# Taking a decode kernel's last output out of PSUM in one VectorE copy, and sending it row by row from partitions 32 apart

## Chip, cores, metric

One core of one Trainium2 chip. The metric is the device time of one execution in microseconds, median of several runs. Runs of one kernel mostly agree within about 0.3%. The experiments ran on several chips, so each is compared with the kernel before in the same rounds. Beside the time, each kernel has one profiled execution with its trace. "SyncE", "ScalarE", "VectorE", "TensorE" and "GpSimd" are SP, ACT, DVE, PE and POOL in the profile's lines. In this kernel TensorE's sums lie in PSUM and all other tiles in SBUF, over up to 128 partitions (rows) each; transfers go between SBUF and HBM. An "issue" is the instruction with which SyncE or ScalarE starts a transfer; DMA engines then move its packets, and it has "landed" when the last update of its semaphore has come.

## The reference

A decode step for two batch rows with 576 features: layer norm, attention over the last 2048 entries of a cache (32 query heads, 16 key and value heads), and beside it a squared-ReLU block, both added to the input.

```python
xn = _layernorm(x, axis=-1)
return x + _A_ref(xn, A_k_cache, A_v_cache, A_wq, A_wo) + _B_ref(xn, B_w1, B_b1, B_w2, B_b2)
# _B_ref: h = xn @ w1 + b1;  r = where(h > 0, h, 0);  out = (r * r) @ w2 + b2      w2: (4608, 576)
# out: (2, 1, 576) bf16
```

Only the very end matters here: the last rows of `w2` are multiplied in, and 2x576 values leave PSUM for HBM.

## The kernel before

B = 2, D = 576, OH = 288, OQ = 144, P = 128, FR = 9. The last weights arrive in two transfers, 7 and 2 of 9 row groups. The last sums are kept in four quarters of 144 columns, one for each 32-partition quadrant of a PSUM bank, with a small matmul for each:

```python
    def mlp_tail(r0, r1):
        w2_sb = w2_tiles.pop((NG4 - 1, r0))
        for r in range(r0, r1):
            o = (r - r0) * D
            for i in range(4):
                pe_mm(mlp["out"][32 * i:32 * i + B, :], lhsT=mlp["h"][:, (NG4 - 1) * FR + r, :],
                                 rhs=w2_sb[:, o + i * OQ:o + (i + 1) * OQ], start=False, stop=(r == FR - 1),
                                 skip_group_check=True, tile_position=(0, 32 * i))
    # ... (cut: the stream of K, V and weights, and everything computed from it)
    mlp["out"] = psum.tile([P, OQ], F32, tag="misc", name="tail_ps")
    for i in range(4):       # the sums so far open the four quarters
        pe_mm(mlp["out"][32 * i:32 * i + B, :], lhsT=ident_f[0:B, 0:B], rhs=part[:, i * OQ:(i + 1) * OQ],
              start=True, stop=False, skip_group_check=True, tile_position=(0, 32 * i))
    mlp_tail(*W2P[NG4 - 1][1:])
    mlp_tail(*W2P[NG4][1:])

    for i, (cp, eng) in enumerate(((nc.vector.tensor_copy, nc.sync), (nc.scalar.copy, nc.scalar))):
        fin_sb = work.tile([B, OH], BF16, tag="fin", name=f"fin_sb_{i}")
        for q in range(2):
            k = 2 * i + q
            cp(out=fin_sb[:, q * OQ:(q + 1) * OQ], in_=mlp["out"][32 * k:32 * k + B, :])
        eng.dma_start(out=out2d[:, i * OH:(i + 1) * OH], in_=fin_sb[:])
```

Of the kernel before, what the change touches and what calls it, by code (L numbers as in the profile page):

```python
# [8 lines left out]
F32 = mybir.dt.float32  # L9
BF16 = mybir.dt.bfloat16  # L10
# [6 lines left out]
def kernel(  # L17
# [14 lines left out]
    nc = tc.nc  # L32
    P = 128
    B, Sq, D = A_x.shape
# [33 lines left out]
    OH = D // 2  # L68
    OQ = D // 4
# [4 lines left out]
    const = ctx.enter_context(tc.tile_pool(name="const", bufs=1))  # L74
# [3 lines left out]
    work = ctx.enter_context(tc.tile_pool(name="work", bufs=2))  # L78
# [3 lines left out]
    def pe_mm(out, **kw):  # L82
        return tc.keep_in_program_order(nc.tensor.matmul(out, **kw))  # L83
# [8 lines left out]
    out2d = out.rearrange("b s d -> (b s) d")  # L92
# [44 lines left out]
    for i in range(2):  # L137
        nc.scalar.dma_start(out=x_sb[B:B + 1, i * OH:(i + 1) * OH],
                            in_=B_b2[i * OH:(i + 1) * OH].rearrange("(o n) -> o n", o=1))
    eps_t = const.tile([B, 1], F32, name="eps_t")  # L140
    nc.vector.memset(eps_t[:], 1e-5)
    warm = const.tile([B, 122], F32, name="warm")
    nc.scalar.activation(out=warm[:, 0:1], in_=eps_t[:], func=ACT.Sqrt)
    for f in issue_kv(k_tiles, A_k_cache, 0, "k"):
        f()
# [12 lines left out]
    ident_f = const.tile([P, P], F32, name="ident_f")  # L158
# [25 lines left out]
    for a in range(2):  # L184
        for r in range(NR2):
# [3 lines left out]
                          in_=pro_ps[:, 0:2 * NR2, :].rearrange("p (a r) b -> p r a b", a=2))  # L189
    nc.vector.tensor_copy(out=xnT[:, 1:HP:2, :, :],  # L190
                          in_=pro_ps[:].rearrange("p (a r) b -> p r a b", a=2)[:, 0:NR2 - 1, :, :])
# [16 lines left out]
                          in_=ident[0:TH, 0:TH].unsqueeze(1).to_broadcast([TH, NT * 32 // TH, TH]))  # L208
    par = const.tile([P, 2, 2, Dh // 2], BF16, name="par")
    for e in range(2):  # L210
        nc.gpsimd.tensor_copy(out=par[:, e, :, :],
                              in_=ident[:, e:Dh:2].unsqueeze(1).to_broadcast([P, 2, Dh // 2]))
# [3 lines left out]
    for k in range(2):  # L216
        for h in range(2):
# [5 lines left out]
                          in_=ident[0:NG4, 0:NG4].unsqueeze(2).to_broadcast([NG4, NG4, B]))  # L223
# [172 lines left out]
    mlp = {}  # L396
# [46 lines left out]
    part = const.tile([B, D], F32, name="part")  # L443
# [107 lines left out]
        cp(out=part[:, i * OH:(i + 1) * OH], in_=out_ps[32 * i:32 * i + B, :])  # L551
    mlp["out"] = psum.tile([P, OQ], F32, tag="misc", name="tail_ps")
    for i in range(4):
        pe_mm(mlp["out"][32 * i:32 * i + B, :], lhsT=ident_f[0:B, 0:B], rhs=part[:, i * OQ:(i + 1) * OQ],
              start=True, stop=False, skip_group_check=True, tile_position=(0, 32 * i))
    mlp_tail(*W2P[NG4 - 1][1:])
    mlp_tail(*W2P[NG4][1:])

    for i, (cp, eng) in enumerate(((nc.vector.tensor_copy, nc.sync), (nc.scalar.copy, nc.scalar))):
        fin_sb = work.tile([B, OH], BF16, tag="fin", name=f"fin_sb_{i}")  # L560
        for q in range(2):
            k = 2 * i + q
            cp(out=fin_sb[:, q * OQ:(q + 1) * OQ], in_=mlp["out"][32 * k:32 * k + B, :])
        eng.dma_start(out=out2d[:, i * OH:(i + 1) * OH], in_=fin_sb[:])


# [28 lines left out]
```

## Time and profile before

| | before |
|---|---|
| time, median of 3 runs | 134.1 us (134.0 to 134.14) |
| span of the profiled run | 132.2 us |
| last weights have landed | 129.09 us after the span's start |
| last cast has signalled | 130.09 us |
| SyncE's output transfer has landed | 131.41 us |

One view is added, busy time in five stretches of the tail: first the stretch, then its length, each engine's busy time with its number of instructions, the granted TensorE clock, the share of the DMA engines, GB/s.

```profile
129.09:130.09 1.00, 0.30 (x8) 0.10 (x7) 0.59 (x2) 0.54 (x2) 0.00 (x0) 1.00 0.00 0
130.09:130.86 0.77, 0.00 (x0) 0.00 (x0) 0.00 (x0) 0.00 (x0) 0.00 (x0) 1.00 0.00 0
130.86:130.96 0.10, 0.00 (x0) 0.00 (x0) 0.00 (x0) 0.00 (x0) 0.00 (x0) 1.00 0.09 23
130.96:131.41 0.45, 0.00 (x0) 0.00 (x0) 0.00 (x0) 0.00 (x0) 0.00 (x0) 1.00 0.00 0
131.41:132.20 0.79, 0.00 (x0) 0.00 (x0) 0.00 (x0) 0.00 (x0) 0.00 (x0) 0.98 0.00 0
```

Of the 3.16 us after the last weights, engines compute in the first microsecond alone. Then come 0.77 us in which transfers are issued, 0.10 us of packets, 0.45 us until they count as landed, and the close.

### The profile page before, as it was taken

What the parts mean: (1) busy time and instruction counts of PE and PEld (TensorE: products, weight loads), DVE (VectorE), ACT (ScalarE), POOL (GpSimd) and SP (SyncE); (2) the same over time, 40 slices, a digit from 0 to 9 for tenths busy, and PEclk for the clock granted to TensorE, in tenths of its full rate; (3) what the DMA queues carried; (4) which work ended last, traced back from release to release, by engine and by line L of the source; (5) the groups of instructions that cost most, each with busy time, mean ns of one, the idle gap of its engine ahead of it and who ended that gap; (6) DMA issues with size and microseconds to landing.
All of it is one profiled execution on the core that took longest, in us unless ns stands there. A gap on an engine that the chain in (4) does not pass through costs nothing.

```text
span 132.2 us, 2040 instructions
## 1 busy us (share of the span) xinstructions
PE 89.0 (67%) x830; PEld 54.7 (41%) x830; DVE 59.1 (45%) x150; ACT 44.2 (33%) x64; POOL 7.7 (6%) x26
## 2 busy tenths in 40 slices
PE   0069319789862967879889389789303996399761
PEld 0059202639521354744466064466003661155540
DVE  6944400224640019246675823778800358644011
ACT  2705401015700226438457145357100751200011
POOL 7700000001000001000010000010000000000000
PEclk9999995955999599689999977999985699959999
DMA  4999989999998999999999999999999999999950
GB/s 154 389 451 479 413 382 431 431 484 477 439 404 350 436 416 441 426 446 416 431 431 426 436 421 439 426 429 431 428 441 416 446 423 422 429 420 433 419 238 1
DMA packets 3632, 53.74 MB, mean 406 GB/s; under 512 B 412, under 2 KB 420, under 8 KB 680
## 3 DMA queue, kind: packets, MB, share of 16 engines
q1 hardware_dynamic: 3604, 53.61, 95.2%
q8 instruction: 6, 0.10, 0.3%
q10 hardware_dynamic: 20, 0.01, 0.0%
q14 instruction: 2, 0.02, 0.0%
HBM read 53.62 MB, written 0.00 MB: 405 GB/s over the span
## 4 chain that ended last, share of the span: by engine, by line
DMA 72%; PE 20%; DVE 2%; ACT 2%; issue 1%; SPq 1%; DVEq 0%; ACTq 0%
DMA k<-in_A_k_cache_dram 44%; DMA w<-in_B_w_dram 14%; DMA wq_sb<-in_A_wq_dram 13%; PE kT_ps L86 10%; PE sc_ps L83 4%; PE q_ps L83 3%; PE pv_ps L83 2%; PE qs_ps L83 1%; DVE kT L286 1%; ACT kT L284 1%; ACT pr L323 1%; PE sm L83 1%; DVE qrow L250 1%; SPq L105 0%; DVE qz L266 0%
## 5 line engine op out<-in xcount | busy, mean ns | idle before, releaser
L86 PE MATMUL kT_ps<-ident_f,k 128*128 128x128 f32 x256 | 41.4, 319 | 12.6 <-DMA k<-in_A_k_cache_dram 12.1
L284 ACT COPY kT<-kT_ps 128x1024 bf16<-128x1024 bf16 x32 | 31.9, 1011 | 36.8 <-PE kT_ps L86 34.0
L86 PEld LDWEIGHTS kT_ps<-ident_f,k 128*128 128x128 f32 x256 | 34.4, 165 | 21.9 <-issue 16.6
L286 DVE COPY kT<-kT_ps 128x1024 bf16<-128x1024 bf16 x32 | 22.1, 691 | 31.9 <-PE kT_ps L86 31.8
L83 PE MATMUL sc_ps<-kT,qz 128*32 128x512 bf16 x128 | 10.7, 418 | 4.5 <-DVE kT L286 2.8
L83 PE MATMUL pv_ps<-v,pT 128*32 128x512 bf16 x128 | 11.7, 435 | 1.0 <-DVE acc L358 0.8
L312 POOL PARTITION_ALL_REDUCE gmax<-m x8 | 2.9, 365 | 103.1 <-DVE m L310 103.1
L323 ACT ACTIVATE pr<-sc_ps,nb 128x512 bf16<-128x512 f32 x8 | 5.5, 687 | 7.9 <-DVE nb L320 7.9
L83 PEld LDWEIGHTS <-xnT 128*4 128x4 bf16 x90 | 2.9, 105 | 11.6 <-issue 11.0
L308 DVE TENSOR_REDUCE mx<-sc_ps 128x1 f32<-128x512 f32 x8 | 5.5, 683 | 3.1 <-PE sc_ps L83 3.1
L83 PE MATMUL q_ps<-wq_sb,xnT 128*4 128x512 bf16 x36 | 3.7, 592 | 4.5 <-DMA wq_sb<-in_A_wq_dram 4.5
L83 PEld LDWEIGHTS <-qz 128*32 128x32 bf16 x128 | 2.3, 98 | 10.1 <-DVE kT L286 6.3
L83 PE MATMUL h_ps<-w_sb,xnT 128*4 128x384 bf16 x54 | 3.9, 420 | 3.4 <-DMA w_sb<-in_B_w_dram 3.4
L358 DVE SCALAR_TENSOR_TENSOR mix<-pv_ps,own_j,mix 128x128 f32<-128x128 f32 x16 | 5.6, 352 | 0.6
L329 DVE STREAM_TRANSPOSE pT<-pr 128x512 bf16<-128x512 bf16 x8 | 5.6, 702 | 0.2 <-ACT pr L323 0.2
L86 PE MATMUL pro_ps<-ident,xs 2*128 2x2 bf16 x10 | 0.6, 164 | 7.6 <-DVE xs L180 7.6
L83 PE MATMUL out_ps<-wo_sb,ws 128*2 128x288 bf16 x64 | 5.1, 323 | 0.3 <-DVE ws L387 0.3
L83 PEld LDWEIGHTS <-pT 128*32 128x32 bf16 x128 | 2.9, 98 | 5.9 <-issue 3.5
L551 ACT COPY part<-out_ps 2x288 f32<-2x288 f32 x1 | 0.4, 389 | 13.5 <-PE out_ps L83 13.5
L83 PE MATMUL sm<-acc,tohead 128*64 128x129 f32 x16 | 3.7, 313 | 1.8 <-DVE acc L358 1.8
L431 DVE TENSOR_TENSOR hs<-hT_ps,hodd 128x20 f32<-128x20 f32 (+1 forms) x4 | 0.5, 172 | 9.2 <-ACT hodd L428 9.2
L83 PE MATMUL out_ps<-w,hT_sb 128*2 128x288 bf16 x54 | 3.8, 286 | 1.1 <-DMA w<-in_B_w_dram 1.1
(78 smaller groups left out, 58.2 us busy)
## 6 DMA issues: line engine op xcount, KB each, us to landing
k<-in_A_k_cache_dram SPq DMA_DIRECT2D x8, 2048.0 KB, 7.7
v<-in_A_v_cache_dram SPq DMA_DIRECT2D x8, 2048.0 KB, 16.9
w_sb<-in_B_w_dram SPq DMA_DIRECT2D x1, 5184.0 KB, 19.3
wq_sb<-in_A_wq_dram SPq DMA_DIRECT2D x1, 4608.0 KB
wo_sb<-in_A_wo_dram SPq DMA_DIRECT2D x2, 2304.0 KB
w<-in_B_w_dram SPq DMA_DIRECT2D x3, 1296.0 KB, 27.2
w<-in_B_w_dram SPq DMA_DIRECT2D x1, 1008.0 KB
w<-in_B_w_dram SPq DMA_DIRECT2D x1, 288.0 KB
```

The source lines that it names most:

```text
L83: return tc.keep_in_program_order(nc.tensor.matmul(out, **kw))
L86: return tc.keep_in_program_order(nc.tensor.transpose(**kw))
L250: nc.vector.tensor_copy(out=qrow[:, 0, :], in_=q_ps[0][0:RB, :])
L284: pin(nc.scalar.copy(out=dst, in_=src))
L286: pin(nc.vector.tensor_copy(out=dst, in_=src))
L308: pin(nc.vector.tensor_reduce(out=mx[:], in_=sc_ps, axis=AX.X, op=ALU.max))
L312: nc.gpsimd.partition_all_reduce(gmax[:], m2[:], channels=P, reduce_op=ReduceOp.max)
L323: pin(nc.scalar.activation(out=pr[:], in_=sc_ps, func=ACT.Exp, bias=nb[:], scale=scale, accum_out=acc[:, Dh:Dh + 1]))
L329: pin(nc.vector.transpose(out=pT[:].rearrange("p t m -> p (t m)"), in_=pr[:]))
L358: op = nc.vector.scalar_tensor_tensor(out=nx, in0=pv_ps[:, j, :], scalar=own_j[:, j:j + 1], in1=acc, op0=ALU.mult, op1=ALU.add)
L431: nc.vector.tensor_tensor(out=hs[:].rearrange("p (g r) b -> p r g b", g=NG4)[:, r0:r0 + n, g:g + 2, :], in0=even[:, :, g:g + 2, :], in1=od ...
L551: cp(out=part[:, i * OH:(i + 1) * OH], in_=out_ps[32 * i:32 * i + B, :])
```

## The change

The intent: one VectorE cast in place of two on each of two engines, on the path that sets the end. For that, all 128 partitions of the PSUM tile must have been written, so the opening matmuls get 32 output rows. The output then sits in partitions 32i + b, and each batch row goes out as four pieces from partitions 32 apart. The spare tile `warm` only keeps the addresses of the later tiles on the same multiple.

```diff
-    warm = const.tile([B, 122], F32, name="warm")
+    warm = const.tile([B, 114], F32, name="warm")
...
-        pe_mm(mlp["out"][32 * i:32 * i + B, :], lhsT=ident_f[0:B, 0:B], rhs=part[:, i * OQ:(i + 1) * OQ],
+        pe_mm(mlp["out"][32 * i:32 * (i + 1), :], lhsT=ident_f[0:B, 0:32], rhs=part[:, i * OQ:(i + 1) * OQ],
...
-    for i, (cp, eng) in enumerate(((nc.vector.tensor_copy, nc.sync), (nc.scalar.copy, nc.scalar))):
-        fin_sb = work.tile([B, OH], BF16, tag="fin", name=f"fin_sb_{i}")
-        for q in range(2):
-            k = 2 * i + q
-            cp(out=fin_sb[:, q * OQ:(q + 1) * OQ], in_=mlp["out"][32 * k:32 * k + B, :])
-        eng.dma_start(out=out2d[:, i * OH:(i + 1) * OH], in_=fin_sb[:])
+    fin_sb = const.tile([P, OQ], BF16, name="fin_sb")
+    nc.vector.tensor_copy(out=fin_sb[:], in_=mlp["out"][:])
+    for b, eng in enumerate((nc.sync, nc.scalar)):
+        eng.dma_start(out=out2d[b:b + 1, :].rearrange("o (i n) -> (o i) n", i=4), in_=fin_sb[b:P:32, :])
```

## The prediction

> **What bounds the kernel now.** I read the page first, for the kind of kernel it is: a decode step that streams 53.6 MB of cache and weights through one core.
>
> ```profile
> span 132.2 us, 2040 instructions
> PE   0069319789862967879889389789303996399761
> DMA  4999989999998999999999999999999999999950
> DMA 72%; PE 20%; DVE 2%; ACT 2%; issue 1%; SPq 1%; DVEq 0%; ACTq 0%
> ```
>
> The second and third of these lines are busy tenths in 40 slices of 3.3 us, the fourth is the chain that ended last. DMA is full until slice 38, and 72% of the chain are transfers. VectorE and ScalarE hold 2% each. The change touches only the last slice and a half, so what counts is the order of events there. Next I read the end of that chain in order of time (start us, us, what):
>
> ```profile
> 109.99 19.10 DMA w<-in_B_w_dram
> 129.09 0.04 issue
> 129.13 0.40 PE tail_ps L83 x8
> 129.53 0.05 ACT fin_sb L563
> 129.58 0.24 issue
> 129.82 0.27 ACT fin_sb L563
> ```
>
> The last weights land at 129.09, eight matmuls on them end at about 129.53, and the casts out of PSUM end at 130.09. The chain stops there, but the span goes on to 132.2, so I read the timeline of the tail (start us, us, engine, line, operation):
>
> ```profile
> 127.80 0.10 PEld L83 LDWEIGHTS tail_ps<-part,ident_f 2*2 2x2 f32 x8 [0.86 <-DVE part L551]
> 127.80 0.42 PE L83 MATMUL tail_ps<-part,ident_f 2*2 2x144 f32 x8 [0.54 <-DVE part L551]
> 128.43 1.00 PE L83 MATMUL tail_ps<-w,hT_sb 128*2 128x144 bf16 x36 [0.20 <-DMA w<-in_B_w_dram]
> 129.46 0.63 DVE L563 CAST fin_sb<-tail_ps 2x144 bf16<-2x144 f32 x2 [1.71 <-PE tail_ps L83]
> 129.52 0.57 ACT L563 CAST fin_sb<-tail_ps 2x144 bf16<-2x144 f32 x2 [1.80 <-PE tail_ps L83]
> 130.11 0.34 SPq L564 DMA_DIRECT2D out_dram<-fin_sb  x1
> 130.12 0.26 ACTq L564 DMA_DIRECT2D out_dram<-fin_sb  x1
> ```
>
> Two casts run on each of two engines side by side, both pairs end at 130.09, and both output transfers are issued within 10 ns of each other. All that follows has nothing beside it. From the packet and semaphore records of the trace: the first output packet starts at 130.86, the last is over at 130.96, the ScalarE queue's transfer has landed at 131.24 and the SyncE queue's at 131.41; from there to the end at 132.25 is the closing exchange among the engines, 0.83 us. So any delay or gain on the SyncE transfer moves the end one for one.
>
> **What the skill says.** "VectorE: DVE Perf Modes", section "The TRN2 errata", prices a copy out of PSUM by the elements in each partition (120 cycles plus elements at 0.96 GHz) and not by partitions; section "Why PSUM operands drop a tier" says an fp32 PSUM source stays at one element per cycle. The trace agrees in kind: the 2x144 cast takes 298 ns, the 2x288 copy of L551 447 ns, that is 149 ns for 144 more elements, or 0.97 elements per ns; the page's formula gives 275 ns for 144, so the trace's 298 is used. "PSUM — Partial Sum Buffer", section "PSUM bank collisions raise a hardware error", says that engines may read one bank together in different 32-partition quadrants; the timeline shows that, with VectorE and ScalarE casting from one bank at once. "DMA: Bandwidth & Descriptors", section "Specifications", says that transfers under 512 B read, modify and write; the old rows are 576 B, the new pieces 288 B. No transfer under 512 B goes out in this trace, so nothing here shows what that costs. "Perfetto Trace Analysis", section "DMA Instruction — HWDGE (DVE, Sync)", says that an issue's recorded time is descriptor generation, with the data movement after it; the trace agrees (issue over at 130.44, packets at 130.86).
>
> **The change, part by part.**
>
> Removed: both ScalarE casts and one VectorE cast. Before, VectorE needs 0.63 us from 129.455 to 130.081. The four quadrants of PSUM are signalled one after another, at 129.431, 129.465, 129.500 and 129.534; the first cast began 24 ns after the first signal. The single new cast reads all quadrants and must wait for the fourth: it begins at 129.534 + 0.024 = 129.558. With 144 elements in each of 128 partitions it takes what 144 elements in 2 partitions took, 0.298, so it ends at 129.856 instead of 130.081. Gain: 0.225 us, not the 0.33 of a whole cast and its gap, since 0.10 of it goes into waiting for the last quadrant. That 128 partitions cost no more than 2 is read from this line, where 128 partitions of 1024 two-byte elements take 691 ns, fewer ns per element than the narrow cast:
>
> ```profile
> L286 DVE COPY kT<-kT_ps 128x1024 bf16<-128x1024 bf16 x32 | 22.1, 691 | 31.9 <-PE kT_ps L86 31.8
> ```
>
> Added on TensorE: the four opening matmuls write 32 rows per quadrant instead of 2, so that every partition read has been written. Still 144 columns stream through, and the weight loads go from 2 to 32 columns, 76 ns each now, perhaps 100 (an estimate between that and the 144 ns of the 128x64 fp32 loads). They end at 128.22, 0.20 us before the next weights land, and a later landing (129.09) decides. Worth nothing.
>
> Moved: the issue of both transfers. Before, one row of 288 elements from each of 2 partitions; after, 144 elements from each of 4 partitions that lie 32 apart. Building both kernels shows a difference the text doesn't: the built program marks transfers whose issue is prepared in advance. In the kernel before, all plain two-dimensional ones bear the mark, the two outputs among them, and the K and V loads do not. In the changed kernel the outputs have lost it. What the mark is worth can be read off the SyncE queue, where transfers issued after a wait compare cleanly:
>
> ```profile
> L105 SPq DMA_DIRECT2D k<-in_A_k_cache_dram x8: 535/544/627, 0.7 to 73.9; - x8
> L129 SPq DMA_DIRECT2D w<-in_B_w_dram x5: 327/328/425, 92.5 to 110.0; - x5
> L564 SPq DMA_DIRECT2D out_dram<-fin_sb x1: 335/335/335, 130.1 to 130.1; - x1
> ```
>
> (minimum/median/maximum ns). Unmarked 535, marked 328 to 335: 0.20 us more. The K loads differ in shape too (128 pieces, three dimensions), so this is an estimate; but the 128-piece marked weight loads take no longer than the 2-piece output, so the number of pieces isn't it. On the SyncE queue the issue becomes about 535 ns, on ScalarE's about 460 (258 + 0.20). The packets start after the issue, so I charge all of it.
>
> Transfer: 4 pieces of 288 B in place of 2 of 576 B for each queue. Old packets took 27 to 33 ns and all eight, completions included, fit in 0.10 us; more of them on more engines is worth 0.0 to 0.03. The smaller writes I charge 0.03 as an unshown risk.
>
> Sum: -0.225 (cast) + 0.20 (issue) + 0.03 (writes) = 0.00 us. New landing about 131.41 as before, span 132.2, time 134.1.
>
> A last part: padding. The spare tile shrinks by 32 bytes and the output tile adds 288 to the constants, so the big buffers shift by 256 bytes and stay 256-byte aligned. I expect no effect on the stream, but it is the only part that could touch 72% of the chain.
>
> **The rivals.**
>
> First, the intended gain comes in full: the lost mark costs nothing, because the 535 ns are due to the K loads' three dimensions. Then the end comes 0.225 us earlier, 133.9. For it: the ScalarE queue's issue of only 258 ns shows issue time varies for reasons I can't name. Against: the mark itself, which separates the queue's clean cases without exception.
>
> Second, small writes into HBM become the new wait: pieces below 512 B[...], written by different engines. The time from packet end to landing is 0.33 us on one queue and 0.45 on the other now; if a read before the write doubled it, the end would be 0.4 later, 134.5. For it: the skill's figure. Against: 576 B is no multiple of 512 either and pays only this; nothing in the trace shows more.
>
> Third, both issues now start on one VectorE signal and contend for a common descriptor generator. But they already start 10 ns apart now. At most the shorter issue queues behind the longer: +0.2, 134.3.
>
> Fourth, the 256-byte shift or a changed rhythm of the stream: tenths of a microsecond either way, with nothing in the profile for it. TensorE's extra rows as a bound I rule out: 0.2 us of slack in front of it, then 0.87 us to the landing that decides.
>
> **Range and chances.** The terms are a firm -0.225 and two soft plusses, so 133.9 to 134.5 covers the rivals; the three runs before spread by 0.14. I take 133.8 to 134.5 around 134.1. Two per cent is 2.7 us, more than all that lies between the last landing and the program's close, so no rival in the tail reaches it; only a disturbed stream could. Faster by 2%: 0.005; within: 0.985; slower: 0.01.
>
> **What would show it.** One VectorE cast 128x144 of 290 to 310 ns that begins about 0.10 us later after the last landing than the first did; issue 0.2 us earlier, relative to that landing; SyncE issue near 535 ns; landing within 0.1 us of the old distance. Wrong: an issue still near 335 (then 133.9), a landing more than 0.5 us after the last packet (small writes), a cast near 600 ns (partitions do cost), or a last weight landing that itself moved by more than 0.3 us (the shift of buffers).

## The result and the profile after

| | before | after |
|---|---|---|
| time, median of 5 runs each | 134.1 us (133.95 to 134.33) | 134.34 us (134.32 to 134.47) |
| span of the profiled run | 132.2 us | 132.5 us |

The ratio after to before is 1.002, 95% interval 1.0005 to 1.0035: within 2%, and very slightly slower. Ratios here are the mean time of one kernel's runs over that of the other's runs of the same rounds, so not quite the ratio of the medians.

The timeline of the tail, changed kernel (start us, us, engine, line, operation, shapes, idle time before it):

```profile
127.76 0.15 PEld L83 LDWEIGHTS tail_ps<-part,ident_f 2*32 2x32 f32 x8 [0.86 <-DVE part L551]
127.76 0.45 PE L83 MATMUL tail_ps<-part,ident_f 2*32 2x144 f32 x8 [0.54 <-DVE part L551]
128.38 1.01 PE L83 MATMUL tail_ps<-w,hT_sb 128*2 128x144 bf16 x36 [0.17 <-DMA w<-in_B_w_dram]
129.44 0.31 DVE L560 CAST fin_sb<-tail_ps 128x144 bf16<-128x144 f32 x1 [1.74 <-PE tail_ps L83]
129.78 0.66 SPq L562 DMA_DIRECT2D out_dram<-fin_sb  x1
129.78 0.61 ACTq L562 DMA_DIRECT2D out_dram<-fin_sb  x1
```

The cast takes half of what the two took, 0.31 us for 0.63. The issues start 0.33 us earlier (0.29 us, counted from the landing of the last weights), but last 0.66 and 0.61 us in place of 0.34 and 0.26. The tail in stretches again, cut at the same events as before:

```profile
129.05:129.76 0.71, 0.29 (x8) 0.10 (x7) 0.31 (x1) 0.00 (x0) 0.00 (x0) 1.00 0.00 0
129.76:131.02 1.26, 0.00 (x0) 0.00 (x0) 0.00 (x0) 0.00 (x0) 0.00 (x0) 0.71 0.00 0
131.02:131.39 0.37, 0.00 (x0) 0.00 (x0) 0.00 (x0) 0.00 (x0) 0.00 (x0) 0.50 0.05 6
```

The stretch with compute went from 1.00 to 0.71 us, the one without anything from 0.77 to 1.26, the one with packets from 0.10 to 0.37. (TensorE has no work in the later stretches, so the lower clock there costs nothing.) Why packets need 0.37 us shows in the rate of the DMA engines, 40 slices of 42.5 ns from 130.5 to 132.2 us; first the kernel before, then the changed one:

```profile
GB/s 0 0 0 0 0 0 0 0 27 14 14 0 0 0 0 0 0 0 0 0 0 0 0 0 0 0 0 0 0 0 0 0 0 0 0 0 0 0 0 0
```

```profile
GB/s 0 0 0 0 0 0 0 0 0 0 0 0 20 7 0 0 0 0 7 21 0 0 0 0 0 0 0 0 0 0 0 0 0 0 0 0 0 0 0 0
```

Before, both queues' packets go out in one burst. After, ScalarE's come in slices 12 and 13 and SyncE's in 18 and 19, 0.27 us later, though both issues began within 5 ns of each other.

So that the arrival of the last weights, which lies between 128.91 and 129.19 us in the traces, doesn't disturb, I count everything from it. From the semaphore and packet records of the two traces, SyncE's transfer:

| step, us | before | after | difference |
|---|---|---|---|
| last weights landed to last cast's signal | 1.002 | 0.709 | -0.293 |
| signal to issue begins | 0.017 | 0.016 | -0.001 |
| issue begins to first packet | 0.799 | 1.519 | +0.720 |
| first to end of last packet | 0.054 | 0.088 | +0.034 |
| end of last packet to landed | 0.452 | 0.330 | -0.122 |
| sum | 2.324 | 2.662 | +0.338 |

From landing to the end of the span it is 0.83 us in both. The spans differ by 0.30 (the weights landed 0.04 earlier in the second), the median times by 0.24.

### The profile page after: what moved, and what is told of

Its sections match the earlier page's. It is cut to its first block, busy times and chain, and to the rows that moved or that the text cites. A ratio compares the mean times of both kernels' runs of the same rounds, so it can differ in the third digit from the quotient of the medians.

```text
span 132.5 us, 2037 instructions
## 1 busy us (share of the span) xinstructions
PE 90.6 (68%) x830; PEld 58.1 (44%) x830; DVE 58.8 (44%) x149; ACT 43.8 (33%) x62; POOL 7.7 (6%) x26
## 4 chain that ended last, share of the span: by engine, by line
DMA 69%; PE 22%; DVE 3%; ACT 1%; issue 1%; SPq 1%; DVEq 0%; ACTq 0%
DMA k<-in_A_k_cache_dram 42%; DMA w<-in_B_w_dram 14%; DMA wq_sb<-in_A_wq_dram 13%; PE kT_ps L86 10%; PE sc_ps L83 4%; PE q_ps L83 3%; PE qs_ps L83 3%; PE pv_ps L83 2%; DVE kT L286 1%; ACT kT L284 1%; ACT pr L323 1%; PE sm L83 1%; DVE qrow L250 1%; SPq L105 0%; DVE qz L266 0%
## 5 line engine op out<-in xcount | busy, mean ns | idle before, releaser
L86 PE MATMUL kT_ps<-ident_f,k 128*128 128x128 f32 x256 | 42.6, 328 | 14.4 <-DMA k<-in_A_k_cache_dram 14.3
L86 PEld LDWEIGHTS kT_ps<-ident_f,k 128*128 128x128 f32 x256 | 36.4, 172 | 22.6 <-issue 21.5
L83 PE MATMUL pv_ps<-v,pT 128*32 128x512 bf16 x128 | 10.7, 400 | 1.0 <-DVE acc L358 0.8
L83 PE MATMUL out_ps<-wo_sb,ws 128*2 128x288 bf16 x64 | 5.9, 354 | 0.3 <-DVE ws L387 0.3
L83 PEld LDWEIGHTS <-ws 128*2 128x2 bf16 x64 | 3.3, 102 | 2.9 <-DVE ws L387 0.6
L83 PEld LDWEIGHTS qs_ps<-sel_q,qrow 100*128 100x128 f32 x16 | 3.5, 330 | 1.8 <-issue 1.8
L83 PE MATMUL qs_ps<-sel_q,qrow 100*128 100x16 f32 x16 | 3.6, 374 | 0.9 <-DVE qrow L250 0.9
```

The source lines that it names most:

```text
L83: return tc.keep_in_program_order(nc.tensor.matmul(out, **kw))
L86: return tc.keep_in_program_order(nc.tensor.transpose(**kw))
```

## The experiments

The theory: the cast is a plain gain of 0.29 us. It is lost because SBUF partitions that are not adjacent cost the transfers the mark for an issue that is prepared in advance (the attribute `ant_dge_precooked` in the built program, below "the mark"), which makes the issue itself longer; and because two unmarked issues that begin together are served one after the other. The rivals: four small pieces are slow in themselves; the new addresses of the big buffers disturb the stream; the cast's gain isn't real. Two numbers are compared: the time, and the distance from the last weights' landing to the landing of the later output transfer (2.324 before, 2.662 after).

**Mark off.** The kernel before, with the mark alone taken away.

```diff
+        nc.dge_precook = False
         eng.dma_start(out=out2d[:, i * OH:(i + 1) * OH], in_=fin_sb[:])
```

> Kernel before, casts and shapes of the transfers untouched; only the build's mark for a prepared issue is taken off both output transfers. Mark theory (the slow issue of the changed kernel comes from the lost mark): SyncE issue goes from 335 ns to 600-680, ScalarE's from 258 to 560-640, the first SyncE packet comes 1.4-1.6 us after its issue starts instead of 0.80, the time rises by 0.6-0.8 us to about 134.8. Shape rival (four strided pieces of 288 B are what is slow): issue stays at 335, time 134.1.

Measured: 134.87 us against 134.13 before (ratio 1.0052, 1.0038 to 1.0066), right result. Its two issues (count, minimum/median/maximum ns):

```profile
L565 SPq DMA_DIRECT2D out_dram<-fin_sb x1: 737/737/737, 130.1 to 130.1; - x1
L565 ACTq DMA_DIRECT2D out_dram<-fin_sb x1: 700/700/700, 130.1 to 130.1; - x1
```

With the same rows, bytes and partitions, issue rises from 335 and 258 ns to 737 and 700. The first packets come 1.336 us after the issue on SyncE and 1.595 on ScalarE, again 0.27 us apart in their bursts:

```profile
GB/s 0 0 0 0 0 0 0 0 0 0 0 0 0 0 0 0 0 0 0 0 0 27 0 0 0 0 0 27 0 0 0 0 0 0 0 0 0 0 0 0
```

This time SyncE is served first. Which of the two is first is not fixed; in each of the four traces with two unmarked issues the other one is later. The distance is 3.001. The mark alone makes both effects; shape isn't needed for either. My expected issue times (600-680 and 560-640) were too short, and SyncE's first packet came before the expected 1.4-1.6 us. The issues are also 0.08 and 0.09 us longer than the changed kernel's 657 and 607; why is open.

**Cast only.** The new cast with the old transfers; `fin_sb` is 128x288 here and zeroed early, and half the output is zeros.

```diff
-    warm = const.tile([B, 114], F32, name="warm")
+    warm = const.tile([B, 42], F32, name="warm")
...
-    fin_sb = const.tile([P, OQ], BF16, name="fin_sb")
-    nc.vector.tensor_copy(out=fin_sb[:], in_=mlp["out"][:])
+    nc.vector.tensor_copy(out=fin_sb[:, 0:OQ], in_=mlp["out"][:])
...
+        eng.dma_start(out=out2d[:, b * OH:(b + 1) * OH], in_=fin_sb[32 * b:32 * b + B, :])
```

> Changed kernel's opening matmuls and single 128-partition cast, but the transfers of before (2 rows of 576 B, marked); the result is wrong on purpose, half of what goes out is zeros. If the cast half of the change is a plain gain: output landing 2.0 us after the last weights' landing instead of 2.32 before, time about 0.29 us under before, 133.8. Rival (the cast gain exists in the trace but a later step swallows it): time within 0.1 of before.

Measured: 133.79 us (ratio 0.9975, 0.9961 to 0.9988), distance 2.036. The cast's gain is real and whole, 0.29 in the trace and 0.34 in the medians. Its lines:

```profile
L561 DVE CAST fin_sb<-tail_ps x1: 308/308/308, 129.4 to 129.4; 128x144 bf16<-128x144 f32 x1
L563 SPq DMA_DIRECT2D out_dram<-fin_sb x1: 335/335/335, 129.7 to 129.7; - x1
```

**Transfers only.** The four old casts, written to partitions 32 apart, and the new transfers; the result is right. The opening matmuls are those of before again.

```diff
...
+    for k, cp in enumerate((nc.vector.tensor_copy, nc.vector.tensor_copy, nc.scalar.copy, nc.scalar.copy)):
+        cp(out=fin_sb[32 * k:32 * k + B, :], in_=mlp["out"][32 * k:32 * k + B, :])
...
```

> The four narrow casts of before, written to partitions 32 apart, and the changed kernel's transfers. Right result. If costs add: before +0.72 (issue to first packet) +0.03 (more packets) -0.12 (shorter landing) = +0.63, time about 134.7. Rival (single signal for both issues is what makes them collide, not their kind): here the SyncE and ScalarE issues start together as well, so it would not separate; if the time is only +0.3 or less, the terms do not add.

Measured: 134.74 us (ratio 1.0046, 1.0033 to 1.0058), distance 3.004. The terms add: -0.29 alone and +0.68 alone give +0.39 together in distance, where the changed kernel shows +0.34. Taken in time, -0.34 and +0.61 give +0.27, where it shows +0.24.

**Lone issue.** The changed kernel, ScalarE's transfer sent early from a zeroed tile; row 1 is wrong.

```diff
...
+    nc.gpsimd.memset(zero[:], 0.0)
+    nc.scalar.dma_start(out=out2d[1:2, :].rearrange("o (i n) -> (o i) n", i=4), in_=zero[1:P:32, :])
...
-    for b, eng in enumerate((nc.sync, nc.scalar)):
+    for b, eng in ((0, nc.sync),):
```

> Changed kernel with the ScalarE transfer sent early from a zeroed tile, so that the SyncE transfer is alone at the end (wrong on purpose: row 1 is zeros). Collision theory (the two unmarked issues share one descriptor generator): SyncE issue falls from 657 ns to 535-600, its first packet comes 1.1-1.25 us after issue start instead of 1.52, time 0.3-0.4 us under the changed kernel, about 134.0. Rival (an unmarked issue costs all of it by itself): 1.5 us stays, time 134.3.

Measured: 134.11 us, level with the kernel before of its rounds (ratio 0.9996, 0.9983 to 1.0008; the changed kernel had 1.002) and 0.23 below the changed kernel's median, distance 2.385.

```profile
L565 SPq DMA_DIRECT2D out_dram<-fin_sb x1: 653/653/653, 129.8 to 129.8; - x1
```

Half of what I expected failed: the issue stays at 653 ns, so its recorded length holds nothing of the collision. But the first packet comes 1.245 us after the issue begins instead of 1.519, and the 0.27 us are gone. Of the 0.72 us lost, 0.45 are the unmarked issue, and 0.27 come from the other queue's transfer beside it.

**Adjacent partitions.** The changed kernel with the partitions' step of 32 made 1; the same four pieces of 288 B go to the same places in HBM, with the wrong rows in them. The built program marks them again.

```diff
-        eng.dma_start(out=out2d[b:b + 1, :].rearrange("o (i n) -> (o i) n", i=4), in_=fin_sb[b:P:32, :])
+        eng.dma_start(out=out2d[b:b + 1, :].rearrange("o (i n) -> (o i) n", i=4), in_=fin_sb[32 * b:32 * b + 4, :])
```

> Changed kernel with one number other: each transfer still moves four pieces of 288 B to the same places in HBM, but reads four adjacent partitions instead of four that lie 32 apart, which brings the mark back (wrong on purpose, the wrong rows go out). Mark theory: SyncE issue about 335 ns, first packet about 0.80 us after issue starts, landing 2.0-2.1 us after the last weights, time 133.8. Rival (four pieces below 512 B cost more in themselves): issue or landing longer, time above 134.0.

Measured: 133.79 us (ratio 0.9983, 0.9967 to 0.9998), distance 2.100.

```profile
L562 SPq DMA_DIRECT2D out_dram<-fin_sb x1: 338/338/338, 129.7 to 129.7; - x1
L562 ACTq DMA_DIRECT2D out_dram<-fin_sb x1: 270/270/270, 129.7 to 129.7; - x1
```

This refutes the shape rival: as many pieces, as small, and issue is back at 338 and 270. Against the cast-only run the four pieces cost 0.06 us of distance (2.100 to 2.036). Building other forms, without running them, the mark was missing whenever the partitions had a step (2, 32 or 64 of them, with two or four pieces), and there for one, two and four adjacent ones.

**Old addresses.** The changed kernel with the spare tile smaller by 256 bytes, so that the big buffers lie where they lay before.

```diff
-    warm = const.tile([B, 114], F32, name="warm")
+    warm = const.tile([B, 50], F32, name="warm")
```

> Changed kernel with the spare tile shrunk by another 256 bytes, so that the big buffers lie where they lay in the kernel before. If the padding is neutral, as predicted: 134.34 as the changed kernel, within 0.1. Rival (the 256-byte shift costs something): 134.1 or less.

Measured: 134.31 us (ratio 1.0014, 0.9999 to 1.0028), where the changed kernel had 134.34 (1.002, 1.0005 to 1.0035): no effect of the shift shows. Here ScalarE's packets come first again, and SyncE's 0.18 us later, not 0.27; so the size of that wait is not fixed. The profiled run shows something else. The granted clock fell during the last matmuls (columns as in the stretches above; the changed kernel has 1.00 in both):

```profile
128.00:129.00 1.00, 0.91 (x28) 0.60 (x24) 0.00 (x0) 0.00 (x0) 0.00 (x0) 0.54 0.20 76
129.00:129.70 0.70, 0.70 (x25) 0.41 (x16) 0.00 (x0) 0.00 (x0) 0.00 (x0) 0.50 0.00 0
```

From the last landing to the cast's signal it took 0.950 instead of 0.709. In three of the traces (this one, four marked, the second of one marked) the clock was 0.50 to 0.61 in this stretch, and in these the step is 0.24 to 0.27 us longer than in its counterpart at 1.00: as much as the whole change. So from here on I compare steps after the casts, where TensorE has no part.

**Four marked transfers.** Right result: the single cast, then one transfer for each quadrant, of two adjacent partitions each.

```diff
-    for b, eng in enumerate((nc.sync, nc.scalar)):
-        eng.dma_start(out=out2d[b:b + 1, :].rearrange("o (i n) -> (o i) n", i=4), in_=fin_sb[b:P:32, :])
+    for i, eng in enumerate((nc.sync, nc.scalar, nc.sync, nc.scalar)):
+        eng.dma_start(out=out2d[:, i * OQ:(i + 1) * OQ], in_=fin_sb[32 * i:32 * i + B, :])
```

> Right result: the single 128-partition cast, and four transfers, one for each PSUM quadrant, of 2 adjacent partitions by 288 B, all marked, two behind each other on each queue. If each marked issue costs 0.34 us and the second one simply follows: last packet about 0.35 us later than in the cast-only run, output landing 2.35-2.45 us after the last weights, time 134.1-134.2, no better than before. Rival (issues of one queue overlap): landing near 2.05, time 133.8.

Measured: 134.29 us (ratio 1.0013, 1.0 to 1.0026), with a clock of 0.50 to 0.61 in the profiled tail. From the cast's signal to the last landing it is 1.639 us, against 1.328 in the cast-only run: the second issue on each queue costs 0.31, all of the cast's gain. No better than before, as expected.

**One marked transfer.** Right result: the old casts into one tile, and one transfer of both rows.

```diff
...
+    fin_sb = const.tile([B, D], BF16, name="fin_sb")
+    for k, cp in enumerate((nc.vector.tensor_copy, nc.vector.tensor_copy, nc.scalar.copy, nc.scalar.copy)):
+        cp(out=fin_sb[:, k * OQ:(k + 1) * OQ], in_=mlp["out"][32 * k:32 * k + B, :])
+    nc.sync.dma_start(out=out2d, in_=fin_sb[:])
```

> Right result: the four narrow casts of before into one tile of 2 rows by 576, one marked transfer of two rows from SyncE. It has no second queue behind whose packets to stand: first packet about 0.75 us after issue starts instead of 0.80, landing 0.32-0.33 us after the last packet instead of 0.45, output landing about 2.15 us after the last weights instead of 2.32, time about 133.95. Rival (the longer landing of SyncE in the kernel before has nothing to do with the other queue): 134.1.

> The one-marked-transfer kernel once more, on the chip of the run above: 133.85 to 133.95, 0.15 to 0.25 us under before. If it is within 0.05 of before, the gain seen first was chance.

Measured: 133.86 us against 134.03 before (ratio 0.9987, 0.9973 to 1.0001), and again 134.18 against 134.08 (1.0009, 0.9997 to 1.0021). The first profiled run had a clock of 1.00 in the tail, the second this:

```profile
128.00:129.00 1.00, 1.00 (x32) 0.62 (x28) 0.00 (x0) 0.00 (x0) 0.00 (x0) 0.50 0.21 81
```

After the casts the two agree: from ScalarE's last cast signal to the landing 1.218 and 1.215 us, where the kernel before takes 1.322 from VectorE's last (its ScalarE signals 7 ns later). So about 0.1 us is gained up to the landing, with 0.326 us from the last packet to the landing in place of 0.452; but the close after it takes 0.89 us in both, where the kernel before takes 0.83, so about half of it is given back. What is left is smaller than what goes with the clock, and the second run, 0.10 us above the kernel before, missed its expectation: in the times no gain is shown.

**Two halves.** Right result: as the last, with two PSUM halves of 288 columns, so that each engine makes one cast.

```diff
...
-            for i in range(4):
-                pe_mm(mlp["out"][32 * i:32 * i + B, :], lhsT=mlp["h"][:, (NG4 - 1) * FR + r, :],
-                                 rhs=w2_sb[:, o + i * OQ:o + (i + 1) * OQ], ...
+            for i in range(2):
+                pe_mm(mlp["out"][32 * i:32 * i + B, :], lhsT=mlp["h"][:, (NG4 - 1) * FR + r, :],
+                                 rhs=w2_sb[:, o + i * OH:o + (i + 1) * OH], ...
...
```

> Right result: as the one-marked-transfer kernel, but the last matmuls write two halves of 288 columns in place of four quarters of 144, so that each engine makes one cast of 2x288 (447 ns on VectorE, about 390 on ScalarE) in place of two of 2x144 (0.63 us). Matmuls of twice the columns end about 0.12 us later; casts end 0.18 earlier: output landing about 2.16 us after the last weights against 2.23, time 133.8, 0.3 under before. Rival (the two column tiles don't run beside each other for long enough, matmuls cost 0.25 more or above): 133.95 or slower than the one-marked-transfer kernel.

Measured: 134.76 us, 134.09 to 135.47 (ratio 1.0061, 1.0026 to 1.0096): a miss. The six runs fall into two groups, three at 134.09 to 134.19, level with the kernel before (134.08), and three at 135.32 to 135.47; the median between them describes neither. The profiled run is of the lower group; what adds 1.2 us in the other is open. The first signal out of TensorE came 0.610 us after the last landing, against 0.341 in the first one-marked run, with a clock of 1.00 in both: 0.27 more, as the rival has it. The chain of the tail shows how; TensorE no longer waits for the weights, but works without a break from 127.90:

```profile
127.90 1.93 PE tail_ps L83 x22
129.83 0.43 DVE fin_sb L561
```

No version here is shown to beat the kernel before. The two whose interval lies below 1 (cast only, adjacent partitions) give wrong results. A transfer from the four quadrants that is one and marked at once I did not find.

## Why the prediction was right or wrong

The time lay in the range, 134.34 in 133.8 to 134.5, and within 2% of the kernel before, as forecast. The argument (a cast's gain that the lost mark gives back) held. Of its sum, two terms were mis-sized (1 and 2), and two were wrongly judged (3 and 4); the rest stood.

1. *The cast, -0.225.* It was -0.293. The cast itself was right: 307 ns for a predicted 298, so 128 partitions cost 9 ns more than 2. (The 691 ns line from which this was read copies 1024 bf16 elements, another type and length, and could not have shown it.) The wait was not: "must wait for the fourth" assumed that the fourth signal stays 0.444 us after the last landing. It came at 0.366, in every run with the single cast and a full clock. In the kernel before, four matmuls signal, 34 ns apart; with one reader only one does, and it came 0.08 earlier than the fourth had. So it seems that the signals had kept the quadrants apart, not the matmuls; no run tests this by itself.
2. *The issue, +0.20.* SyncE's issue grew by 0.322 (335 to 657), ScalarE's by 0.349, and mark-off alone makes it 0.40 and 0.44. The K loads' 535 ns were a poor stand-in, though the K and V loads were the only unmarked issues in the old trace. And "the packets start after the issue, so I charge all of it" left out that the packets start later after an unmarked issue's end too: alone, 1.245 us lie between issue and first packet, 0.45 more than before's 0.80, of which the issue accounts for 0.32.
3. *The third rival, set aside.* "They already start 10 ns apart now" was the wrong comparison: marked issues hardly get in each other's way (first packets 47 ns apart, and SyncE's 0.799 us after its issue beside the other against 0.752 alone, in one marked transfer), unmarked ones do (0.18 to 0.27). The rival was real and about as large as its 0.2 or larger, and the lone-issue run gives 0.23 us of time back for it. But the delay does not show in the length of the issue, so that it lies in the generator is not shown.
4. *Small writes, +0.03.* The packets took 0.034 more; landing took 0.122 less, which was not foreseen. SyncE's transfer lands 0.33 us after its last packet when no other queue's packets went just before it (changed kernel, lone issue, one transfer) and 0.45 to 0.48 when they did (before, cast only, adjacent). By moving the queues' packets apart, the collision gave a part back.
5. *Rows on TensorE and padding: nothing.* The weight loads went from 0.10 to 0.15 us in all with a wait of 0.17 us for the next weights still behind them; old addresses gave the same time.

Sum 0.00, measured +0.34 in the trace and +0.24 in the time. That this still fell into the range is due to the rivals being in it, and in part to luck: the larger loss on the issues (0.72 for 0.20) was partly made up by a larger gain on the cast and a shorter landing that nobody had foreseen. One remark was wrong as it stands: 2.7 us is not "more than all that lies between the last landing and the program's close"; from the last weights it is 3.16 us, of which the change could touch the 2.32 up to the output's landing. The first rival (full gain) is refuted by mark-off, the second (small writes) by adjacent partitions and by the changed kernel itself, whose landing took 0.330 us.

## What to carry to other kernels

An operation that is cheaper on an engine can leave its data in a layout that makes the next transfer dearer: count from the last input's arrival to the output's landing, not to the end of the last compute, and look in the built program at what became of the transfers. Output rows in adjacent partitions kept their issue at a third of a microsecond here; stepped ones took two thirds, and when two of them were issued together, the later one's packets came another 0.18 to 0.27 us later. When a tail is decided by tenths of a microsecond, look at the granted clock there before believing a difference in the medians.

## What the Trainium skill lacked or had wrong

- "DMA: Bandwidth & Descriptors" has one kind of plain hardware-issued transfer on this chip. The runs show two: output transfers took SyncE 257 to 338 ns and ScalarE 254 to 270 ns with the mark, 653 to 737 and 606 to 700 without; in the programs built here a step between SBUF partitions takes the mark away. No page has this.
- "Perfetto Trace Analysis", section "DMA Instruction — HWDGE (DVE, Sync)", says that the generator is locked for one user and that the profile's issue time includes waiting for it. The later of two unmarked issues had its packets 0.18 to 0.27 us later, but the issue time did not show the wait: 657 ns beside another, 653 alone. Where the wait lies is open.
- "DMA: Bandwidth & Descriptors", section "Specifications", warns of reading and rewriting below 512 B. Four writes of 288 B landed 0.33 us after the last packet (lone issue), two of 1152 B 0.33 (one marked transfer): no delay shows for writes this few.
- "VectorE: DVE Perf Modes", section "The TRN2 errata", gives 275 ns by its formula for 144 fp32 elements out of PSUM; the casts took 298 ns from 2 partitions and 307 or 308 from 128.
